# Attention batches 3 to 7: 32x32 block turns on VectorE in place of TensorE transposes, attention pieces behind the second product, and a later place for the pair splits

## The chip, the cores and the metric

The kernel runs on one core of one Trainium2 chip. The metric is device time in microseconds (us), of one launch. Engines are named as in the profile: PE is TensorE's matmul stream and PEld its weight loads, DVE is VectorE, ACT is ScalarE, POOL is GpSimd, SP is SyncE, which here issues every DMA.

## What is computed

Attention in both directions between 512 tokens and 32 states, in 8 batches of 8 heads, then two feed-forward blocks on the 8 x 544 = 4352 rows that result:

```python
scores = scale * x @ state.T          # (B,H,S,Ns) = (8,8,512,32), D = 64
a = softmax(scores, -1); xread = a @ state
a2 = softmax(scale * state @ x.T, -1); sread = a2 @ x
h0 = concat([xread, sread], axis=2)   # -> rows (4352, 512)
h1 = (relu(h0 @ w_in) ** 2) @ w_out   # w_in 512x2048, w_out 2048x512
out = (((h1 @ w1) * (h1 @ w2)) @ w3) @ w_out2
```

The weights arrive as 64-bit floats. Products run in the fp32r type, with each operand split into a high and a low part and three passes (HI,HI), (LO,HI), (HI,LO), so one product of a 128x128 weight tile takes three matmuls.

## The kernel before, in words

**First half: attention and the first block.** The work is cut into chunks c: chunks 0 to 7 are the 512 tokens of a batch, chunk 8 is the 256 state rows of all batches. For each of the 16 tiles f of 128 hidden columns, `h_tile(c, f)` (L375) makes the hidden tile with 6 matmuls of 512 columns (products of `SW`, which is state times w_in, with the turned attention weights `aT`), `act_h` (L367) does relu and square on ScalarE and the split into HI (ScalarE, L83) and LO (VectorE, L84), and `y_tile` (L410) adds the tile's part to the four output banks with 12 matmuls. `y_tile` runs two tiles behind `h_tile` (the list `pend`, L578). The main loop is at L558; its index i counts (c, f), and from i = 32 on i = 16 c + f.

Between `h_tile` and `y_tile` of iteration i the loop runs `side[i]` (L562), a table written by hand. For each batch b it holds, in the iterations of chunk b - 1: the attention pieces of batch b in the slots of `att_slots` (L336); `make_sw` (L349) in slots 1, 5, 9 and 13, 16 matmuls that fill the two banks of tag "m"; every second iteration one `conv`, which makes fp32 out of one 512 KB block of 64-bit weights with five VectorE instructions and one on ScalarE (`convert64`, L123), stores it, and loads a later block; and two x loads with their copies on GpSimd. The raw blocks and the raw x tiles share three buffers (tag "raw").

The attention pieces of one batch on TensorE are: `xpose` four times (four 128x128 transposes of x against the identity, L228), `scores` (16 matmuls into both "m" banks, L240), `soft1a` twice (four transposes of the scores S, so that the row softmax over the 32 states runs along a row, L268), `a_T` twice (four transposes back, L288), `a2_T` twice (L297), `sread` twice (16 small matmuls, L305) and `sread_T` twice (one transpose, L319). All use the two "m" banks. The slots are L340 to L345: xpose 0 to 3, scores 4, a2_T 6 and 10, soft1a 7 and 11, sread 8 and 11, sread_T 9 and 12, a_T 10 and 13.

`tc.issue_after(ins)` (L561) queues each instruction that the block traces on the engine of `ins` behind `ins`; here `done[i - 3]`, the VectorE half of a hidden tile's split. The rest of the order on each engine is made by the scheduler from the order of the program.

**Second half.** Eight token chunks go in four pairs, twice (s = 0 and 1, for the two halves of the 1024 columns; the second pass takes the pairs in reverse). For each pair `quad` (L714) runs four times, 42 matmuls each: seven products of sums and differences of the operands take the place of eight, and VectorE puts the results together. Then come eight output tiles `out_tile` (L793) of 12 matmuls. The operands Y of the next pair are loaded by `load_pair` (L667, two buffers of tag "wi1") and made by `make_pair` (L680): 14 splits, each one cast on ScalarE and one subtraction on VectorE (L84), and 8 differences on VectorE (L693). Chunks 0 and 1 were written in three parts, so for the pair (0, 1) `load_pair` also loads the other parts and adds them on GpSimd (L676). `load_pair` is called after quad m = 1 (L848), `make_pair` after the first output tile (L862). The scheduler may place the VectorE work of `make_pair` earlier than where it is called.

## Time and profile before

| | us |
|---|---|
| median of 3 runs (lowest, highest) | 1330.67 (1328.37, 1331.24) |
| the profiled execution, its own time | 1329.5 |
| its span, first to last instruction | 1327.7 |
| PE busy | 1284.6 (97%) |
| PEld busy | 1012.7 (76%) |
| DVE busy | 782.9 (59%) |
| ACT busy | 654.8 (49%) |
| POOL busy | 64.5 (5%) |
| DMA, share of the 16 engines' span | 30.5% |
| mean granted clock of TensorE | 0.985 |

The profiled execution is 1.2 us shorter than the median. Spans on TensorE are modelled and overlap, so the time of a piece is read here from the start of one instruction to the start of the next. The clock is a share of 2.4 GHz; 0.50 is 1.2 GHz.

### The profile page before, as it was taken

To read this page: it belongs to the slowest core of one execution; us is meant where nothing else is said; L and a number is where in the kernel's file an instruction comes from. 1 tells how busy PE (TensorE), PEld (TensorE's weight loads), DVE (VectorE), ACT (ScalarE), POOL (GpSimd) and SP (SyncE) were. 2 spreads that over 40 slices of the span, in tenths; PEclk is the share of its full clock that TensorE was granted. 3 is DMA by queue.
4 is the path that set the end of the run, shared out by engine and by line. 5 is a ranking of instruction groups with operands and counts; after the bars stand their busy time and mean duration, and the time that the engine had idled before them with its cause. 6 is when DMAs were issued, how large, how long until landed. Compare 5 with 4: busy or idle time off the path is not lost.

```text
span 1327.7 us, 17120 instructions
## 1 busy us (share of the span) xinstructions
PE 1284.6 (97%) x6552; PEld 1012.7 (76%) x6552; DVE 782.9 (59%) x1388; ACT 654.8 (49%) x1190; POOL 64.5 (5%) x52
## 2 busy tenths in 40 slices
PE   3998999999999999999999999999799999999998
PEld 2666677777777777777789988888688888888877
DVE  6899875565656656543244764736273747567552
ACT  3765765656556565554565633525153533425121
POOL 0112300000000000000000000000500000000000
PEclk8898999999999999999999999999899999999999
DMA  6246534233242332300031342031502235050322
GB/s 205 65 129 223 172 103 135 96 103 104 81 149 72 105 117 80 103 9 1 33 127 64 108 162 79 18 110 60 179 32 96 78 129 163 28 191 9 119 70 89
DMA packets 65361, 132.70 MB, mean 100 GB/s; under 512 B 8704, under 2 KB 17408, under 8 KB 64768
## 3 DMA queue, kind: packets, MB, share of 16 engines
q1 hardware_dynamic: 65280, 131.62, 30.5%
q8 instruction: 51, 0.84, 0.2%
q14 instruction: 30, 0.25, 0.1%
HBM read 88.08 MB, written 43.52 MB: 99 GB/s over the span
## 4 chain that ended last, share of the span: by engine, by line
PE 86%; DVE 7%; DMA 3%; ACT 2%; issue 1%; POOL 1%; SPq 0%; POOLq 0%; DVEq 0%
PE y L419 25%; PE po L799 12%; PE qa L718 9%; PE qd L718 6%; PE ps_sw L354 3%; PE ps_w L603 3%; PE qc L718 3%; PE qe L718 3%; PE ab L773 2%; DMA yp<-yscr 1%; PE ps_r L309 1%; PE ps_x L232 1%; DVE ce L143 1%; DVE cm L140 1%; DVE ghl L84 1%
## 5 line engine op out<-in xcount | busy, mean ns | idle before, releaser
L419 PE MATMUL y<-ghl,wo 128*128 128x512 f32 (+1 forms) x1728 | 414.6, 386 | 5.4 <-ACT yo L428 5.0
L419 PEld LDWEIGHTS y<-ghl,wo 128*128 128x128 f32 x1728 | 304.8, 189 | 103.2 <-issue 24.7
L84 DVE TENSOR_TENSOR ghl<-r,ghl 128x512 fp32r<-128x512 f32 (+1 forms) x144 | 96.8, 672 | 150.7 <-ACT ghl L83 129.9
L718 PE MATMUL qa<-yq,wq 128*128 128x512 f32 x576 | 144.9, 390 | 0.0
L726 ACT COPY s<-qa 128x512 f32<-128x512 f32 x96 | 56.4, 588 | 146.7 <-PE qa L718 141.0
L718 PEld LDWEIGHTS qa<-yq,wq 128*128 128x128 f32 x576 | 108.5, 188 | 22.7
L718 PE MATMUL qd<-yq,wq 128*128 128x512 f32 x384 | 99.5, 393 | 8.3 <-ACT s L726 8.3
L799 PE MATMUL po<-w34b,c 128*128 128x512 f32 x408 | 95.9, 390 | 0.3 <-DVE o L808 0.3
L799 PE MATMUL po<-w,c 128*128 128x512 f32 x408 | 95.6, 390 | 0.0
L718 PEld LDWEIGHTS qd<-yq,wq 128*128 128x128 f32 x384 | 72.8, 190 | 23.9 <-ACT s L726 8.7
L371 ACT ACTIVATE r<-r 128x512 f32<-128x512 f32 (+1 forms) x144 | 88.2, 612 | 2.3
L799 PEld LDWEIGHTS po<-w34b,c 128*128 128x128 f32 x408 | 76.3, 188 | 17.1 <-DVE o L808 0.8
L799 PEld LDWEIGHTS po<-w,c 128*128 128x128 f32 x408 | 76.2, 188 | 16.4 <-ACT o L805 0.8
L83 ACT CAST ghl<-r 128x512 fp32r<-128x512 f32 (+1 forms) x144 | 86.2, 599 | 3.3
L136 ACT ACTIVATE ce<-ce,ebias 128x512 int32<-128x512 int32 x72 | 51.9, 724 | 31.2 <-DVE ce L135 31.0
L354 PE MATMUL ps_sw<-win,stT 64*32 64x512 f32 (+1 forms) x528 | 55.9, 595 | 1.6 <-DVE aT L84 0.8
L730 DVE TENSOR_TENSOR s<-qa,s 128x512 f32<-128x512 f32 x32 | 22.1, 690 | 59.3 <-ACT s L726 59.3
L143 DVE SCALAR_TENSOR_TENSOR ce<-raw,ce 128x512 int32<-128x512 int32 x72 | 50.9, 708 | 4.1 <-ACT ce L136 4.0
L140 DVE SCALAR_TENSOR_TENSOR cm<-raw,cm 128x512 f32<-128x512 uint32 x72 | 52.9, 735 | 0.6
L83 ACT CAST c<-s 128x512 fp32r<-128x512 f32 x64 | 38.9, 621 | 28.8 <-DVE s L747 28.2
L83 ACT CAST yq<-yraw 128x512 fp32r<-128x512 f32 x70 | 42.1, 624 | 16.0 <-PE qa L718 7.5
L718 PE MATMUL qc<-yq,wq 128*128 128x512 f32 x192 | 50.0, 396 | 0.0
(542 smaller groups left out, 1851.0 us busy)
## 6 DMA issues: line engine op xcount, KB each, us to landing
raw<-in_moe_w_dram SPq DMA_DIRECT2D x32, 512.0 KB, 4.1
yraw<-yscr SPq DMA_DIRECT2D x56, 256.0 KB, 4.7
raw<-in_moe_w_out_dram SPq DMA_DIRECT2D x24, 512.0 KB, 3.7
yscr<-yo SPq DMA_DIRECT2D x48, 256.0 KB, 3.0
oscr<-o SPq DMA_DIRECT2D x34, 256.0 KB, 3.0
opart<-oscr SPq DMA_DIRECT2D x34, 256.0 KB, 3.5
x<-in_x_dram SPq DMA_DIRECT2D x16, 512.0 KB, 4.0
out_dram<-o SPq DMA_DIRECT2D x32, 256.0 KB, 2.8
```

Source lines behind the costliest of these rows:

```text
L83: nc.scalar.copy(hi, src)
L84: return nc.vector.tensor_tensor(out=lo, in0=src, in1=f32(hi), op=ALU.subtract)
L136: nc.scalar.activation(e, e, ACTF.Relu, bias=ebias, scale=8.0)
L140: nc.vector.scalar_tensor_tensor(out=f32(m), in0=lw, scalar=2.0**-32, in1=m, op0=ALU.mult, op1=ALU.add)
L143: nc.vector.scalar_tensor_tensor(out=e, in0=hw, scalar=-(2**31), in1=e, op0=ALU.bitwise_and, op1=ALU.bitwise_or)
L354: nc.tensor.matmul(pss[r][k * NS:(k + 1) * NS, cols], stT[rows, b, k, :], win_t[fg][rows, k, cols], start=True, stop=True, tile_position=( ...
L371: nc.scalar.activation(r[:, :n], r[:, :n], ACTF.Square)
L419: nc.tensor.matmul(y_ps[c, d][:, :n], wo_t[f][:, wi, d * P:(d + 1) * P], t[:, gi, :n], start=(f == f0 and k == 0), stop=(f == f1 - 1 and k ...
L603: nc.tensor.matmul(ps, t[:, wi, (j % 4) * P:(j % 4 + 1) * P], wo2_t[j][:, vi, :], start=(j == 0 and k == 0), stop=(j == N1 - 1 and k == 2),)
L718: nc.tensor.matmul(ps, W[w, kt][:, wi, m * P:(m + 1) * P], Y[v, kt][:, vi, :], start=(first and kt == 0 and k == 0), stop=(last and kt == ...
L726: nc.scalar.copy(t, ps)
L799: nc.tensor.matmul(ps, v[:, vi, t * P:(t + 1) * P], w[:, wi, :], start=(m == 0 and k == 0), stop=(m == QM - 1 and k == 2),)
```

## The change

For batches 3 to 7 (`b >= BLK`) x is loaded twice. `load_xb` loads it in pieces of 32 tokens by 32 columns, so that VectorE's 32x32 block transpose (`turn_x`) gives the turned x; `load_xn` loads it straight into the tile X that `sread` reads, with the tokens in natural order. `xpose`, its copies on ScalarE and GpSimd's copies of x go. `soft1a` turns S in 32x32 blocks on VectorE, which leaves the 32 states along the row, and `a_T` turns the weights back on VectorE, into the buffer of S. The slots are moved up, since no turn of x stands ahead of the scores. The output rows of chunks 3 to 7 are stored in natural order.

For batches 2 to 7 the attention pieces move from `side` to `late`: they are issued behind `y_tile` and not between `h_tile` and `y_tile`.

In the second half `load_pair` is called after quad m = 0, and what `make_pair` and `make_w` put on VectorE is queued behind the last VectorE instruction of the pair's quads.

```diff
@@ -54,6 +54,7 @@
     HI, LO = 0, 1
+    BLK = 3
@@ -217,6 +218,33 @@
+    xT = {}
+    def load_xb(b, g):
+        t = raw_tile(False, f"xb{b}_{g}").bitcast(F32).rearrange("p a b -> p (a b)")
+        for r in range(2):
+            for a in range(2):
+                p0 = (2 * r + a) * NS
+                for k in range(2):
+                    nc.sync.dma_start(
+                        t[p0:p0 + NS, k * 512:(k + 1) * 512].rearrange("p (c i) -> p c i", i=NS),
+                        x[b, g * HG + 2 * k + r, :, a * NS:(a + 1) * NS].rearrange("(c p) i -> p c i", p=NS),
+                    )
+        raws["xb", b, g] = t
+    def turn_x(b, g):
+        raw = raws.pop(("xb", b, g))
+        for k in range(2):
+            t = att.tile([P, 512], F32, tag="xT", bufs=4, name="xT")
+            nc.vector.transpose(out=t, in_=raw[:, k * 512:(k + 1) * 512])
+            xT[b, 2 * g + k] = t
+    def load_xn(b, g):
+        t = att.tile([P, HG, J, D], F32, tag="X", bufs=2, name=f"X{b}_{g}")
+        nc.sync.dma_start(t, x[b, g * HG:(g + 1) * HG].rearrange("h (j p) d -> p h j d", p=P))
+        X[b, g] = t.rearrange("p h j d -> p j h d")
@@ -235,7 +263,7 @@
             nc.scalar.copy(t, ps)
-            v["xT", k] = t
+            xT[b, k] = t
@@ -243,7 +271,7 @@
                     nc.tensor.matmul(
-                        pss[r][k * NS:(k + 1) * NS, :], stT[rows, b, k, :], v["xT", k][rows, :],
+                        pss[r][k * NS:(k + 1) * NS, :], stT[rows, b, k, :], xT[b, k][rows, :],
                         start=True, stop=True, tile_position=(r * D, k * NS),
@@ -266,13 +294,17 @@
         def soft1a(r):
-            ps = bank_m("ps_n")
-            for j in range(J):
-                nc.tensor.transpose(ps[:, j * P:(j + 1) * P], v["S", r][:, j * P:(j + 1) * P], ident)
-            pv = ps.rearrange("p (k n) -> p k n", n=NS)
+            e = att.tile([P, J * HG, NS], F32, tag="e1", bufs=1, name="e1")
+            if b >= BLK:
+                nc.vector.transpose(out=e.rearrange("p k n -> p (k n)"), in_=v["S", r])
+                pv = e
+            else:
+                ps = bank_m("ps_n")
+                for j in range(J):
+                    nc.tensor.transpose(ps[:, j * P:(j + 1) * P], v["S", r][:, j * P:(j + 1) * P], ident)
+                pv = ps.rearrange("p (k n) -> p k n", n=NS)
             mx = att.tile([P, J * HG, 1], F32, tag="mx", bufs=2, name="mx")
             nc.vector.tensor_reduce(out=mx, in_=pv, axis=AX.X, op=ALU.max)
-            e = att.tile([P, J * HG, NS], F32, tag="e1", bufs=1, name="e1")
             nc.vector.tensor_tensor(out=e, in0=pv, in1=mx.to_broadcast([P, J * HG, NS]), op=ALU.subtract)
@@ -286,10 +318,14 @@
         def a_T(r):
-            ps = bank_m("ps_a")
             e = v["e1", r].rearrange("p k n -> p (k n)")
-            for j in range(J):
-                nc.tensor.transpose(ps[:, j * P:(j + 1) * P], e[:, j * P:(j + 1) * P], ident)
+            if b >= BLK:
+                ps = v["S", r]
+                nc.vector.transpose(out=ps, in_=e)
+            else:
+                ps = bank_m("ps_a")
+                for j in range(J):
+                    nc.tensor.transpose(ps[:, j * P:(j + 1) * P], e[:, j * P:(j + 1) * P], ident)
             t = pa.tile([P, 2, 512], F32R, tag=f"aT{r}", bufs=2, name=f"aT{r}")
@@ -337,6 +373,12 @@
         xp, sc, s2, s1a, s1b, at, a2t, sr, srt = att_steps(b)
+        if b >= BLK:
+            return [
+                [sc], [], [s2[0], s1a[0]], [],
+                [s1b[0], s2[1]], [a2t[0]], [at[0], s1a[1]], [sr[0]],
+                [s1b[1], srt[0]], [a2t[1]], [at[1]], [sr[1]], [srt[1]], [], [], [],
+            ]
         return [
@@ -505,6 +547,7 @@
     side = {i: [] for i in range(NF * B)}
+    late = {}
     side[0] = [lambda: make_win0(1, 0), s2[0], lambda: make_win0(1, 1), xp1[0], xp1[1], a2t[0]]
@@ -521,13 +564,18 @@
         for i, steps in enumerate(att_slots(b)):
-            side[(b - 1) * NF + i] = steps + side[(b - 1) * NF + i]
+            late[(b - 1) * NF + i] = steps
         for fg in range(NFG):
...
             i = 9 + g if b == 2 else (b - 2) * NF + 12 + g
-            side[i].append(lambda b=b, g=g: (load_x(b, g), make_x(b, g)))
+            if b < BLK:
+                side[i].append(lambda b=b, g=g: (load_x(b, g), make_x(b, g)))
+            else:
+                side[i - 4].append(lambda b=b, g=g: load_xb(b, g))
+                side[i - 2].append(lambda b=b, g=g: turn_x(b, g))
+                side[i + 2].append(lambda b=b, g=g: load_xn(b, g))
     for _ in range(3):
@@ -578,6 +626,9 @@
             y_tile(*pend.pop(0))
+        with tc.issue_after(done[i - 3].ins) if i >= 8 else nullcontext():
+            for job in late.get(i, ()):
+                job()
@@ -708,8 +759,8 @@
         t = bp.tile([P, 2, 512], F32R, tag="c", bufs=2 * QM, name="c")
-        split(t[:, HI, :n], t[:, LO, :n], q)
         c_t[c, m] = t
+        return split(t[:, HI, :n], t[:, LO, :n], q)
@@ -748,7 +799,7 @@
         nc.vector.tensor_tensor(out=p1, in0=p1, in1=u3, op=ALU.mult)
-        to_c(c0, m, p1, 512)
+        return to_c(c0, m, p1, 512)
@@ -807,7 +858,8 @@
         if c < B:
-            dst = out[c * T:c * T + S, :].rearrange("(p j) e -> j p e", j=J)[t]
+            rows_t = "(p j) e -> j p e" if c < BLK else "(j p) e -> j p e"
+            dst = out[c * T:c * T + S, :].rearrange(rows_t, j=J)[t]
             nc.sync.dma_start(dst, o)
@@ -844,8 +896,8 @@
             for m in range(QM):
-                quad(c0, c1, m)
-                if m == 1 and i + 1 < len(todo):
+                last = quad(c0, c1, m)
+                if m == 0 and i + 1 < len(todo):
                     raw = load_pair(*todo[i + 1])
@@ -859,10 +911,11 @@
                 out_tile(c, t, s)
-                if n == 0 and i + 1 < len(todo):
-                    make_pair(raw)
-                if n == 0 and i + 1 == len(todo) and s == 0:
-                    make_w(raw)
+                with tc.issue_after(last.ins):
+                    if n == 0 and i + 1 < len(todo):
+                        make_pair(raw)
+                    if n == 0 and i + 1 == len(todo) and s == 0:
+                        make_w(raw)
                 if n == 3 and i + 1 == len(todo) and s == 1:
...
             if s == 0 and i + 1 == len(todo):
```

**How the order moves.** TensorE, tiles 0 to 2 of chunk 4, while batch 5's attention is worked on (ph is the hidden tile, y an output bank, ps_x the turned x, ps_s the scores, ps_sw the product of `make_sw`). Before:

```order
L383 MATMUL ph_0__3578<-aT_3340,sw_3494 128x512 x3
L383 MATMUL ph_0__3578<-aT_3481,sw_3497 128x512 x3
L232 MATMUL ps_x<-ident,X_0_3449 128x128 x4
L419 MATMUL y_2976<-ghl,wo_1648 128x512 x3
...
L383 MATMUL ph_1__3622<-aT_3340,sw_3494 128x512 x3
L383 MATMUL ph_1__3622<-aT_3481,sw_3497 128x512 x3
L232 MATMUL ps_x<-ident,X_0_3449 128x128 x4
L354 MATMUL ps_sw<-win_660,stT 32x512 x8
L419 MATMUL y_2976<-ghl,wo_1662 128x512 x3
```

Now:

```order
L425 MATMUL ph_0__3556<-aT_3166,sw_3472 128x512 x3
L425 MATMUL ph_0__3556<-aT_3365,sw_3475 128x512 x3
L461 MATMUL y_2969<-ghl,wo_1641 128x512 x3
...
L461 MATMUL y_2972<-ghl,wo_1641 128x512 x3
L273 MATMUL ps_s<-xT,stT 32x512 x8
L425 MATMUL ph_1__3607<-aT_3166,sw_3472 128x512 x3
L425 MATMUL ph_1__3607<-aT_3365,sw_3475 128x512 x3
L396 MATMUL ps_sw<-win_660,stT 32x512 x8
L461 MATMUL y_2969<-ghl,wo_1655 128x512 x3
```

The transposes are gone, the scores stand behind the output product, and a hidden tile stands between an attention piece and the next ps_sw.

VectorE in the second half, first pass, around the quads of the pair (6, 7), with what each row waits for (yraw, ytmp and yq belong to the splits of the next pair; s and c to the quads). Before:

```order
L84 TENSOR_TENSOR yq<-yraw,yq 128x512 [waits PE_49]
L693 TENSOR_TENSOR ytmp<-yraw 128x512 [waits Pool_49]
L693 TENSOR_TENSOR yraw<-yraw 128x512 [waits DVE_49,Pool_49]
L730 TENSOR_TENSOR s_8462<-qe,s_8462 128x512 [waits PE_49]
L730 TENSOR_TENSOR s_8485<-qd,s_8485 128x512 [waits PE_49,Activation_49]
L693 TENSOR_TENSOR ytmp<-yraw 128x512 [waits Pool_49]
L730 TENSOR_TENSOR s_8470<-qa,s_8470 128x512 [waits Activation_49]
```

Now:

```order
L801 TENSOR_TENSOR s_8608<-s_8608,s_8652 128x512 [waits DVE_49]
L85 TENSOR_TENSOR c<-s_8631,c 128x512 [waits Activation_49]
L85 TENSOR_TENSOR c<-s_8608,c 128x512 [waits Activation_49]
L85 TENSOR_TENSOR yq<-yraw,yq 128x512 [waits Pool_49] x2
L744 TENSOR_TENSOR ytmp<-yraw 128x512
L744 TENSOR_TENSOR ytmp<-yraw 128x512 [waits Pool_49]
```

The rows that wait for GpSimd stood among the first quad's rows; now they stand behind the last quad's two splits of c.

TensorE in the second pass, from a pair's first output tile to the next pair's quads (po is an output tile, qa, qd, qe and qc are the banks of a quad). Before:

```order
L799 MATMUL po<-w34b,c 128x512 x12
L718 MATMUL qd<-yq,wq 128x512 x3
L718 MATMUL qe<-yq,wq 128x512 x6
L799 MATMUL po<-w34b,c 128x512 x60
L718 MATMUL qa<-yq,wq 128x512 x6
```

Now:

```order
L850 MATMUL po<-w34b,c 128x512 x20
L769 MATMUL qa<-yq,wq 128x512
L850 MATMUL po<-w34b,c 128x512 x4
L769 MATMUL qa<-yq,wq 128x512 x4
L850 MATMUL po<-w34b,c 128x512 x12
L769 MATMUL qa<-yq,wq 128x512
L769 MATMUL qd<-yq,wq 128x512 x6
L769 MATMUL qe<-yq,wq 128x512 x6
L769 MATMUL qa<-yq,wq 128x512 x12
...
L850 MATMUL po<-w34b,c 128x512 x60
```

The whole first quad of the next pair now stands behind 36 matmuls of output tiles and ahead of the other 60; before, 9 matmuls of it stood there. In the first pass almost all of it stays behind all eight output tiles.

## Rows read from the trace of the kernel before

**Rows 1.** Profile page, part 1: busy us (share) x instructions, each engine.

```profile
PE 1284.6 (97%) x6552; PEld 1012.7 (76%) x6552; DVE 782.9 (59%) x1388; ACT 654.8 (49%) x1190; POOL 64.5 (5%) x52
```

**Rows 2.** Windows: stretch, us, busy PE PEld DVE ACT POOL (x), PEclk, DMA, GB/s.

```profile
131.50:216.20 84.70, 82.95 (x444) 60.77 (x444) 64.13 (x122) 53.72 (x97) 14.49 (x8) 1.00 0.43 141
216.20:624.60 408.40, 408.36 (x2212) 304.14 (x2211) 231.86 (x448) 237.23 (x417) 9.59 (x8) 1.00 0.28 88
624.60:694.30 69.70, 69.57 (x338) 54.22 (x337) 23.62 (x37) 39.37 (x68) 0.00 (x0) 1.00 0.21 76
```

**Rows 3.** Timeline of PE, chunk 4: start us, us; hidden tiles 1 to 14.

```profile
384.20 1.52 PE L383 MATMUL ph__3622<-aT,sw 128*128 128x512 f32 x6
...
390.76 1.52 PE L383 MATMUL ph__3682<-aT,sw 128*128 128x512 f32 x6
...
395.31 1.52 PE L383 MATMUL ph__3730<-aT,sw 128*128 128x512 f32 x6
...
399.87 1.52 PE L383 MATMUL ph__3762<-aT,sw 128*128 128x512 f32 x6
...
405.20 1.52 PE L383 MATMUL ph__3813<-aT,sw 128*128 128x512 f32 x6
...
410.55 1.53 PE L383 MATMUL ph__3865<-aT,sw 128*128 128x512 f32 x6
...
415.12 1.53 PE L383 MATMUL ph__3909<-aT,sw 128*128 128x512 f32 x6
...
419.69 1.52 PE L383 MATMUL ph__3954<-aT,sw 128*128 128x512 f32 x6
...
425.02 1.52 PE L383 MATMUL ph__4008<-aT,sw 128*128 128x512 f32 x6
...
431.15 1.53 PE L383 MATMUL ph__4053<-aT,sw 128*128 128x512 f32 x6
...
446.07 1.52 PE L383 MATMUL ph__4201<-aT,sw 128*128 128x512 f32 x6
...
453.01 1.52 PE L383 MATMUL ph__4254<-aT,sw 128*128 128x512 f32 x6
...
457.09 1.52 PE L383 MATMUL ph__4291<-aT,sw 128*128 128x512 f32 x6
```

**Rows 4.** Lines of DVE in chunk 4: count, busy us, mean ns, idle before.

```profile
L274 DVE TENSOR_REDUCE mx<-ps_n 128x16 f32<-128x512 f32 x2 | 1.4, 692 | 1.7 <-PE ps_n L271 1.7
```

**Rows 5.** Lines of POOL, whole span.

```profile
L176 POOL TENSOR_TENSOR wo<-cw,wo 128x512 fp32r<-128x512 f32 x16 | 25.9, 1618 | 99.3 <-ACT wo L175 89.5 <-DMA raw<-in_moe_w_in_dram 9.8
```

**Rows 6.** DMA queues, 1.5 to 4.0 us (only state loads): packets, MB, share.

```profile
q1 hardware_dynamic: 717, 0.16, 29.2%
```

**Rows 7.** Timeline of SP at the start: eight state loads.

```profile
0.74 3.69 SPq L440 DMA_DIRECT2D st<-in_state_dram  x8
```

**Rows 8.** Timeline of PE, chunk 1, with waits in brackets.

```profile
159.69 1.57 PE L354 MATMUL ps_sw<-win,stT 64*32 64x512 f32 x16 [0.71 <-ACT S L251]
...
166.57 0.66 PE L300 MATMUL ps_a<-ident,e 128*128 128x128 f32 x4 [0.98 <-DVE sw L84]
```

**Rows 9.** Windows of two pairs' periods in the second half, columns as in rows 2.

```profile
935.50:1006.70 71.20, 62.88 (x265) 51.34 (x264) 37.72 (x57) 26.72 (x48) 15.31 (x12) 0.93 0.37 118
1129.20:1189.10 59.90, 59.90 (x266) 49.56 (x264) 38.88 (x62) 20.83 (x38) 0.00 (x0) 1.00 0.33 106
```

**Rows 10.** Timeline of PE, first pass, quads of the pair (6, 7).

```profile
957.56 2.92 PE L718 MATMUL qd<-yq,wq 128*128 128x512 f32 x6 [8.32 <-ACT s L726]
```

**Rows 11.** Timeline of DVE in the same stretch.

```profile
953.67 0.69 DVE L693 TENSOR_TENSOR ytmp<-yraw 128x512 f32<-128x512 f32 x1 [8.83 <-POOL yraw L676]
```

**Rows 12.** Timeline of PE where the pair (4, 5) passes to output tiles.

```profile
912.26 4.24 PE L799 MATMUL po<-w,c 128*128 128x512 f32 x18
```

**Rows 13.** Timeline of DVE in the same stretch.

```profile
916.18 1.28 DVE L84 TENSOR_TENSOR c<-s,c 128x512 fp32r<-128x512 f32 x2
```

**Rows 14.** Windows: the end of the wait of rows 10 and what followed.

```profile
957.50:963.40 5.90, 5.84 (x14) 4.58 (x15) 3.44 (x4) 1.21 (x3) 2.42 (x3) 0.50 0.23 70
```

## The prediction

> **What bounds the kernel now.** I read the page's busy times first: TensorE is busy 97% of the span, the next engine 59% [rows 1]. What TensorE issues, and the few gaps in it, sets the time. Next the windows by stage: chunks 2 to 6, in which batches 3 to 7 get their attention, take 408.40 us, all of it TensorE busy, so 81.68 each; chunk 7, with no attention beside it, takes 69.70; chunk 1, with batch 2's attention, 84.70 [rows 2]. Attention therefore costs about 12 us a chunk on the engine that binds. Then TensorE's timeline of one chunk, read from one hidden tile's start to the next [rows 3]: the reader is to see that an iteration with nothing beside it lasts 4.08 us (453.01 to 457.09), and by how much each piece makes it longer. Last the second half: a pair's period is 59.90 us, one of them is 71.20 [rows 9].
>
> The sum below is made against the profiled execution's 1329.5 us. The median of the runs stands 1.2 higher, and I add that at the end. A measurement of this kernel can tell some 0.2% (2.7 us) from no change.
>
> **First half, batches 3 to 7.** Per batch 32 transposes leave TensorE: four groups of four for x, two for `soft1a`, two for `a_T`. One group costs 0.48 us (395.31 to 399.87 is 4.56, against 4.08) [rows 3]. Eight groups are 3.84 us.
>
> There is a second saving. A `make_sw` alone adds 1.27 us (405.20 to 410.55). Where it follows an attention piece directly, the two cost more than their sum, since both want the two "m" banks: with an x group 2.48 (384.20 to 390.76), 0.73 too much; with `sread_T`, taken as 0.12, a quarter of a group, 2.05 (425.02 to 431.15), 0.66 too much; with an `a_T` group 2.86 (446.07 to 453.01), 1.11 too much [rows 3]. That is 2.50 per batch. In the new order a hidden tile stands between an attention piece and each `make_sw`, and no piece follows another directly.
>
> What stays, built up from the plain chunk: 69.70 holds three `make_sw`; add a fourth (1.27), the scores (399.87 to 405.20, 1.25), two `a2_T` groups (410.55 to 415.12, 0.49 each), two `sread` (419.69 to 425.02, 1.25 each) and two `sread_T` (0.12 each): 75.94 us [rows 2, 3]. That is 5.74 less than 81.68, **28.7 us less in five chunks**. (The two savings add to 6.34; the plain chunk has 0.6 us of waits of its own, 69.70 less 16 x 4.08 and 3 x 1.27, which I leave in.)
>
> What could eat it:
> - *VectorE.* It gets eight block turns a batch. No row shows one. The ends are nothing and 1.62 us, the slowest 128x512 pass of any engine, GpSimd's subtraction [rows 5]. I take 0.69, VectorE's own row reduction, a pass of the same size with one source [rows 4]. VectorE is busy 231.86 / 5 = 46.4 us a chunk [rows 2]; with eight turns that is 51.9 of 75.9, with the upper end 59.3. It is covered; without cover it would cost its 5.5 us a batch. A turn would have to take 3.7 us before VectorE filled the chunk.
> - *The scores before a `make_sw`.* Both banks of the scores must be copied by ScalarE before the next `make_sw`, one hidden tile (1.36 of the 4.08) later. Between nothing and the 0.73 of the x group I take 0.3 a batch, **+1.5 us**.
> - *The x loads.* Each batch issues 16 block loads and two of X on SP in place of two. Eight small loads of the state hold SP 3.69 us [rows 7], so 16 hold it some 7.4, once a chunk, with weight loads and stores behind. The pieces are of 128 bytes, 4096 for each half of a batch. State pieces of 256 bytes take 29.2% of 16 engines over 2.5 us for 717, or 16.3 ns [rows 6]; 4096 of them are 4.2 us on 16 engines. The ends are half of that (half the bytes) and 20 us. I take 4.2 and cost it at nothing: the turn of the second half stands three hidden-tile splits later in VectorE's order than the conversion that frees its buffer, some 13 us.
> - *The Trainium skill, "DMA: Bandwidth & Descriptors", Specifications,* gives 512 bytes as the least size for full rate, below which the engine reads, modifies and writes. If that doubled a piece's time, a half would need 8.4 us, still inside the 13; the sum is the same by row and by rule, but this is why the last rival below gets 5% and not 2%.
> - ScalarE loses four copies a batch and GpSimd two; neither binds, so that gives nothing.
>
> **First half, batch 2.** It keeps its transposes, only behind the output product. Chunk 1 shows two plain waits, 0.71 and 0.98, of attention work for data that was not yet ready [rows 8], and has the same adjacent pieces as above, 2.50. At most 4.2 goes; the order is new, so nothing may go, or waits of the same 1.7 may appear. I take **-3.0 us**.
>
> **Second half.** The long period is that of the pair (6, 7): 71.20 against 59.90 [rows 9]. TensorE waits 8.32 us for ScalarE [rows 10], which waits for VectorE, which stands 8.83 us at a difference of the pair (0, 1) until GpSimd has added the parts [rows 11]. Afterwards the granted clock is 0.50, that is 1.2 GHz, for the rest of the first quad [rows 14]; six matmuls take 2.92 there. In the new order these differences stand behind the last quad's splits, so VectorE cannot be held inside the quads: **-11.3 us**. GpSimd's additions then have the whole 38 us of the quads; the load starts when `make_pair` of (6, 7) has freed its buffers.
>
> What is late next is `make_pair`. VectorE's last splits of c end at 917.46, 5.2 us after the quads [rows 12, 13]. Behind them come 22 instructions, at 0.64 each (1.28 for two) [rows 13] 14.1 us, so the last operand is ready 19 us after the quads. In the first pass eight output tiles, 96 matmuls at 0.227 (18 in a plain iteration of 4.08) [rows 3], cover 21.8 us, which is enough. In the second pass the next quad starts after only 42 matmuls, 9.5 us. It asks for its operands in the order in which they are made and needs the last kind some 8 us in, at 17.7 us. So up to 1.5 us is late, perhaps nothing, perhaps 2.5 with the output additions in between. I take 0.6 for each of three such passages: **+1.8 us**.
>
> **Sum.** 1329.5 - 28.7 + 1.5 - 3.0 - 11.3 + 1.8 = 1289.8; with the 1.2 to the median, **1291.0 us**.
>
> **The rivals.**
> 1. *Collisions move and do not go.* The pieces behind the output product hold the "m" banks just as long; the scores come closer to a `make_sw`, and VectorE empties other banks later in a fuller queue. Then the 2.50 a batch stays, and batch 2 gains nothing: 1291.0 + 12.5 + 3.0 - 1.5 = **1305**. For it: the waits of rows 8 are of this kind. Against it: a whole hidden tile now stands in between.
> 2. *The passages in the second pass bind.* If each makes TensorE wait 4 us, at the ratio of the known wait (11.3 lost for 8.32) that is 16.3 in place of 1.8: **1305.5**. For it: the order puts a whole quad early. Against: operands come in the order of use.
> 3. *Slower.* The block loads land so late that VectorE stands at a turn, with the hidden tiles' splits behind it. TensorE has two tiles in hand, 8 us, on top of the 13. With a wait like the known one in each of five batches the cost is 56.5: **1347.5**. To lose all of the 39.7 gained, a batch must lose 7.9, a wait of 5.8 at that ratio, so a half must land over 27 us after its issue, more than six times the 4.2.
>
> That the change does not do what it says can be left out: the rows of the new order show the transposes gone and the pieces moved.
>
> **How the numbers follow.** My forecast 0.69 (1283 to 1299), rival 1 0.15, rival 2 0.09, rival 3 0.05, something that cancels the gain almost exactly 0.02. The lower end, 1283, is the sum without the two allowances (3.3), with batch 2's full 4.2 and the plain chunk's own waits gone (3.0). The upper end takes in rivals 1 and 2 and half of their overlap: 1309. Faster by over 0.2%: 0.93; within: 0.02; slower: 0.05.
>
> **What would show it.** Right: no TensorE rows of x turns in chunks 2 to 6, each of these chunks near 76 us, block turns near 0.7, `make_sw` iterations near 5.35 everywhere, no pair's period above 61 us, clock 1.00 through the second half. Wrong: chunks of 78 or more with all transposes gone (rival 1), 62 to 66 us periods in the second pass (rival 2), or VectorE waiting for x loads in the list of waits (rival 3).

## The result and the profile after

The changed kernel takes **1299.22 us** (median of 4 runs, 1298.32 to 1300.17), the kernel before 1330.49 in the runs beside it: ratio 0.9768, 95% interval 0.9751 to 0.9785. That is 31.3 us less. The forecast was 39.7 less and 1291.0; the time lies 8 us above it, inside the range of 1283 to 1309.

The profiled execution took 1299.79 us, its span 1298.0. Page, part 1, and the windows of the stretches that [rows 2] show of before (chunk 1, chunks 2 to 6, chunk 7):

```profile
PE 1255.5 (97%) x6392; PEld 988.4 (76%) x6392; DVE 801.2 (62%) x1428; ACT 651.6 (50%) x1170; POOL 57.4 (4%) x42
```
```profile
132.70:222.80 90.10, 85.22 (x459) 61.09 (x458) 67.35 (x125) 55.71 (x99) 12.04 (x6) 0.98 0.51 139
222.80:602.10 379.30, 377.60 (x2035) 284.23 (x2034) 247.04 (x484) 228.28 (x395) 0.00 (x0) 1.00 0.40 106
602.10:671.80 69.70, 69.60 (x337) 54.21 (x337) 23.62 (x37) 39.20 (x68) 0.00 (x0) 1.00 0.23 76
```

Chunks 2 to 6 went from 408.40 to 379.30, chunk 7 did not move, and **chunk 1 grew**, from 84.70 to 90.10. Chunks 3 to 6 are 76.06 each; chunk 2 is 75.09, because the scores of batch 3 (1.0) have moved ahead of its first hidden tile. Like for like, chunk 1 is 4.4 longer and five chunks 28.1 shorter. Chunk 1 differs between executions: in three others with this first half (experiments 8 to 10) it is 90.3, 91.0 and 92.3.

TensorE's timeline of chunk 4, the starts of hidden tiles as in [rows 3]:

```profile
373.96 1.52 PE L425 MATMUL ph__3556<-aT,sw 128*128 128x512 f32 x6
...
379.15 1.65 PE L425 MATMUL ph__3607<-aT,sw 128*128 128x512 f32 x6
...
384.61 1.52 PE L425 MATMUL ph__3660<-aT,sw 128*128 128x512 f32 x6
...
393.39 1.52 PE L425 MATMUL ph__3742<-aT,sw 128*128 128x512 f32 x6
397.47 1.52 PE L425 MATMUL ph__3796<-aT,sw 128*128 128x512 f32 x6
...
403.33 1.64 PE L425 MATMUL ph__3844<-aT,sw 128*128 128x512 f32 x6
```

An empty iteration is 4.08 still (393.39 to 397.47). Scores and the `make_sw` after them take 5.19 and 5.46, together 2.49 more than two empty ones, no more than their own 1.25 and 1.27. A `make_sw` with an `a2_T` behind the output product adds 1.78 (397.47 to 403.33), their sum of 1.76 again. No piece pays for its neighbour any more. The turns, in VectorE's lines of chunks 2 to 6:

```profile
L240 DVE STREAM_TRANSPOSE xT<-xb 128x512 f32<-128x512 f32 x16 | 10.8, 697 | 0.1
L324 DVE STREAM_TRANSPOSE S<-e 128x512 f32<-128x512 f32 x10 | 7.1, 705 | 0.0
L299 DVE STREAM_TRANSPOSE e<-S 128x512 f32<-128x512 f32 x10 | 7.0, 703 | 0.0
```

Now chunk 1. One wait of TensorE stands out; its timeline, then those of ScalarE and VectorE, and the window behind it:

```profile
158.18 1.09 PE L273 MATMUL ps_s<-xT,stT 64*32 64x512 f32 x16
159.20 1.65 PE L425 MATMUL ph__1553<-aT,sw 128*128 128x512 f32 x6
164.31 2.44 PE L396 MATMUL ps_sw<-win,stT 64*32 64x512 f32 x16 [3.46 <-ACT S L279]
```
```profile
159.97 0.61 ACT L176 CAST wo<-cw 128x512 fp32r<-128x512 f32 x1
163.15 0.62 ACT L176 CAST wo<-cw 128x512 fp32r<-128x512 f32 x1 [2.57 <-DVE cw L147]
163.67 1.06 ACT L279 COPY S<-ps_s 128x512 f32<-128x512 f32 x2
```
```profile
161.56 1.56 DVE L147 SCALAR_TENSOR_TENSOR cw<-cm,ce 128x512 f32<-128x512 f32 x1
```
```profile
164.40:167.80 3.40, 3.40 (x19) 1.21 (x20) 2.33 (x8) 3.37 (x8) 0.72 (x1) 0.50 0.03 11
```

The scores of batch 2 begin at 158.18, and the hidden tile behind them at 159.20. The two copies of S that free the "m" banks stand on ScalarE behind two casts of converted weights; the second waits 2.57 us for VectorE's conversion. `make_sw`, the next to want the banks, starts 3.46 us late, and for 3.4 us after it the granted clock is 0.50. In the order before, the copies stood ahead of those casts. The Trainium skill, "PSUM — Partial Sum Buffer", Engine vs sequencer instructions, says that ScalarE's queue is strictly first in, first out; the copies' start at 163.67, behind a cast that had nothing to do with them, agrees.

The second half, against 59.90 and 71.20 in [rows 9]. Each window goes from one pair's first output tile to the next pair's. The second one holds the quads of the pair (6, 7), where the long wait was, the third those of the pair (0, 1); the last three are the second pass:

```profile
829.90:889.90 60.00, 60.00 (x265) 49.33 (x264) 34.00 (x54) 26.42 (x46) 0.00 (x0) 1.00 0.21 70
889.90:949.90 60.00, 60.00 (x265) 49.34 (x264) 36.32 (x54) 26.43 (x46) 21.79 (x16) 1.00 0.42 132
949.90:1010.20 60.30, 60.30 (x265) 49.23 (x265) 34.00 (x54) 24.03 (x42) 0.00 (x0) 1.00 0.20 70
1070.20:1132.10 61.90, 60.58 (x265) 48.97 (x265) 38.80 (x62) 21.78 (x38) 0.00 (x0) 1.00 0.31 102
1132.10:1193.20 61.10, 60.64 (x266) 48.97 (x265) 38.80 (x62) 21.77 (x38) 0.00 (x0) 1.00 0.31 104
1193.20:1253.60 60.40, 60.40 (x266) 48.92 (x265) 38.80 (x62) 18.34 (x32) 0.00 (x0) 1.00 0.23 74
```

The long period is gone and the clock is 1.00 in all of them; the one behind it is 60.3, and the three periods of the second pass have grown by 2.0, 1.2 and 0.5.

### The profile page after: what moved, and what is told of

It reads as the page before. It is cut to its first block, busy times and chain, and to the rows that moved or that the text cites. A ratio compares the mean times of both kernels' runs of the same rounds, so it can differ in the third digit from the quotient of the medians.

```text
span 1298.0 us, 16933 instructions
## 1 busy us (share of the span) xinstructions
PE 1255.5 (97%) x6392; PEld 988.4 (76%) x6392; DVE 801.2 (62%) x1428; ACT 651.6 (50%) x1170; POOL 57.4 (4%) x42
## 4 chain that ended last, share of the span: by engine, by line
PE 83%; DVE 8%; DMA 4%; ACT 3%; issue 1%; SPq 0%; POOL 0%; DVEq 0%; ACTq 0%; POOLq 0%
PE y L461 24%; PE po L850 12%; PE qa L769 10%; PE qd L769 6%; PE ps_w L654 3%; PE qc L769 3%; PE qe L769 3%; PE ps_sw L396 2%; PE ab L824 2%; PE ps_r L345 1%; DMA out_dram<-o 1%; DMA x<-in_x_dram 1%; DVE ghl L85 1%; DVE sw L85 1%; DMA yscr<-yo 1%
## 5 line engine op out<-in xcount | busy, mean ns | idle before, releaser
L461 PE MATMUL y<-ghl,wo 128*128 128x512 f32 (+1 forms) x1728 | 408.5, 383 | 8.9 <-ACT yo L470 7.7
L461 PEld LDWEIGHTS y<-ghl,wo 128*128 128x128 f32 x1728 | 309.6, 189 | 101.1 <-ACT r L411 17.6
L727 POOL TENSOR_TENSOR yraw<-yraw,yp 128x512 f32<-128x512 f32 x16 | 21.8, 1362 | 760.5 <-DMA oscr<-o 745.6
L859 DVE TENSOR_TENSOR o<-po,opart 128x512 f32<-128x512 f32 x34 | 23.4, 690 | 46.4 <-PE po L850 35.9
L141 DVE SCALAR_TENSOR_TENSOR cm<-raw,cm 128x512 f32<-128x512 uint32 x72 | 49.9, 693 | 0.8
```

The source lines that it names most:

```text
L141: nc.vector.scalar_tensor_tensor(out=f32(m), in0=lw, scalar=2.0**-32, in1=m, op0=ALU.mult, op1=ALU.add)
L461: nc.tensor.matmul(y_ps[c, d][:, :n], wo_t[f][:, wi, d * P:(d + 1) * P], t[:, gi, :n], start=(f == f0 and k == 0), stop=(f == f1 - 1 and k ...
```

## The experiments

Times are medians; each run had the kernel before beside it (1329.7 to 1330.6). "Chunk" lengths are those from one chunk's first hidden tile to the next one's, read from the trace.

**1 and 2. The wait in chunk 1.** First, the order of the casts alone:

```diff
+    s_copy = {}
...
-                nc.scalar.copy(s, pss[r])
+                s_copy[b] = nc.scalar.copy(s, pss[r])
...
-            for job in side.get(i, ()):
-                job()
+            with tc.issue_after(s_copy[2].ins) if i == 22 else nullcontext():
+                for job in side.get(i, ()):
+                    job()
```

> The changed kernel with one order added: the two weight conversions of iteration 22 are queued on ScalarE behind batch 2's two copies of S. Theory A (chunk 1 grew because those copies stood behind two casts of weights that wait for VectorE, so that make_sw found its banks full for 3.5 us and the clock then fell): TensorE's wait of 3.46 us at 161 us goes, no clock of 0.50 follows, chunk 1 goes from 90.1 to about 84.6, the kernel from 1299.2 to about 1293.7. Rival (the late place of batch 2's pieces costs by itself, or the block loads and turns of batch 3 that begin in chunk 1 do): another wait takes its place, chunk 1 stays within 1.5 of 90, the kernel at 1298 to 1299.

Second, batch 2's pieces back in their old place:

```diff
-            late[(b - 1) * NF + i] = steps
+            if b < BLK:
+                side[(b - 1) * NF + i] = steps + side[(b - 1) * NF + i]
+            else:
+                late[(b - 1) * NF + i] = steps
```

> The changed kernel with batch 2's pieces back between hidden tile and output product; batches 3 to 7 as changed. Theory A: the scheduler's old order comes back with the old place, the copies of S ahead of the casts, chunk 1 about 85 to 86 (84.7 as before, and 1.0 for batch 3's scores if they stay there), the kernel 1294 to 1295. Rival (block loads and turns of batch 3 in chunk 1): they are still there, chunk 1 stays at 89 to 90, the kernel at 1299.

Windows of chunk 1, of the first and then of the second:

```profile
132.40:217.60 85.20, 83.20 (x460) 60.59 (x459) 67.14 (x126) 55.21 (x99) 12.02 (x6) 1.00 0.52 148
```
```profile
132.60:220.80 88.20, 85.80 (x459) 61.28 (x458) 66.29 (x125) 54.72 (x99) 11.81 (x6) 1.00 0.51 144
```

The first gives 1292.80 us (ratio 0.9717, 0.9702 to 0.9731): chunk 1 goes from 90.1 to 85.2, the wait and the clock of 0.50 are gone. Theory A holds: about 5 us of the miss is the place of two casts. The second gives 1294.49, but its chunk 1 is 88.2, not the 85 to 86 expected: the old waits of [rows 8] are back (0.8 and 1.0), and something new remains near its end. So the late place itself is good for batch 2, and there is a second loss.

**3. The second loss: scores drawn forward.** In chunk 1 of experiment 1 the scores of batch 3 take 3.65 us in place of 1.02, behind an `a_T` of batch 2, and 42 matmuls of the output product follow in a row. The edit queues these scores behind the output product:

```diff
...
-            y_tile(*pend.pop(0))
+            y_last = y_tile(*pend.pop(0))
...
-            for job in late.get(i, ()):
-                job()
+            with tc.issue_after(y_last.ins) if i == 32 else nullcontext():
+                for job in late.get(i, ()):
+                    job()
```

> The first experiment's kernel (conversions of iteration 22 behind the copies of S) with a second order: on TensorE the scores of batch 3 stand behind the output product that is written ahead of them. Theory A2 (what is left of the miss in chunk 1 is that these scores were drawn forward by more than one hidden tile, directly behind an a_T of batch 2 that holds the same banks: 3.65 us for what takes 1.02): the collision of 2.6 goes, 1.0 moves from chunk 1 to chunk 2, chunk 1 goes from 85.15 to about 81.5 and chunk 2 from 75.1 to 76.1, the kernel from 1292.8 to about 1290.2. Rival (the scores are late there because their operands are, and would wait as long in any place): 85.15 + 75.08 = 160.2 stays within 0.7, the kernel at 1292.8.

1292.74 us, no change; chunks 1 and 2 are 159.6 in place of 160.2. The rival was right: the time is waited for elsewhere, now in the output product. TensorE's timeline:

```profile
200.59 0.96 PE L462 MATMUL y<-ghl,wo 128*128 128x512 f32 x3 [1.16 <-ACT yo L471]
202.61 9.14 PE L462 MATMUL y<-ghl,wo 128*128 128x512 f32 x39 [1.06 <-DVE yo L469]
```

Two output banks had not been copied out (`yo`, two buffers). Why is on SyncE, whose timeline in the changed kernel reads (there all of this stands some 6 us later than in the run above):

```profile
182.35 14.56 SPq L230 DMA_DIRECT2D xb<-in_x_dram  x16
197.01 0.91 SPq L471 DMA_DIRECT2D yscr<-yo  x2
```

The first two copies are done at 190.5 (ScalarE 188.83, VectorE 189.82), and their stores wait behind sixteen block loads until 197.0. The other two copies need the same buffers; in the order that was made around this they stand on ScalarE and VectorE behind the splits of aT and two block turns, at 206.0 and 208.0. Before the change these stores were issued from 184.73 on, as soon as the first copy (184.10, 0.60 long) had ended.

**4. The loads off SyncE.** On top of experiment 1:

```diff
-                    nc.sync.dma_start(
+                    (nc.gpsimd if b == 3 else nc.sync).dma_start(
```

> The first experiment's kernel (conversions of iteration 22 behind the copies of S) with the sixteen block loads of batch 3 issued by GpSimd in place of SyncE. Theory A3 (they hold SyncE for 14.2 us, the stores of the output copies yo behind them go 7 us late, the two copies that need the same buffers stand 14 us late behind the splits of aT and the block turns, and their output banks hold TensorE up, first in the scores of batch 3 and, when these were moved, in the output product itself): the stores go within 2 us of their copies, the output products no longer bunch (42 in a row), no wait of the scores or of the output product above 0.8 from 195 us on; chunks 1 and 2 together go from 160.2 to about 157.6, the kernel from 1292.8 to about 1290.2. Rival (a_T of batch 2 and the scores of batch 3 collide in the m banks whatever SyncE does): chunks 1 and 2 stay at 160, the kernel at 1292.8. Other rival (loads issued by GpSimd land late and the turns hold VectorE): a wait of VectorE for xb, 1294 or more.

SyncE, and the window of chunk 1:

```profile
183.16 3.16 SPq L472 DMA_DIRECT2D yscr<-yo  x3
...
189.09 0.32 SPq L472 DMA_DIRECT2D yscr<-yo  x1
```
```profile
132.20:214.50 82.30, 79.79 (x443) 59.93 (x442) 67.20 (x125) 54.63 (x97) 22.45 (x22) 1.00 0.52 157
```

The stores follow their copies, the output products no longer bunch, and the scores are back in chunk 2 (76.05). Chunks 1 and 2 are 158.4, 1.8 less than in experiment 1 and not the 2.6 expected: one output product still waits 1.6 us at 187 us for a `yo` copy, which waits for the buffer of the store before. And only half of the 1.8 belongs to the loads. TensorE, in experiment 1 and then here, at an earlier wait for a `yo` copy, at batch 2's scores, and at the second hidden tile of chunk 2, which in both stands behind batch 3's scores:

```profile
147.24 1.79 PE L462 MATMUL y<-ghl,wo 128*128 128x512 f32 x6 [1.59 <-ACT yo L471]
158.31 1.09 PE L274 MATMUL ps_s<-xT,stT 64*32 64x512 f32 x16
221.64 1.52 PE L426 MATMUL ph__2175<-aT,sw 128*128 128x512 f32 x6
```
```profile
146.27 1.70 PE L462 MATMUL y<-ghl,wo 128*128 128x512 f32 x6 [0.87 <-ACT yo L471]
157.25 1.09 PE L274 MATMUL ps_s<-xT,stT 64*32 64x512 f32 x16
219.70 1.65 PE L426 MATMUL ph__2175<-aT,sw 128*128 128x512 f32 x6
```

The first wait is over before any block load is issued (from 177 us on), and it differs from execution to execution whatever the order (1.42 in experiment 12, which has both repairs). From the scores to the hidden tile it is 63.33 in experiment 1 and 63.36 in experiment 3, against 62.45 here and 62.5 in experiments 11 and 12. So **the loads on SyncE cost 0.9**. The run does not separate their hold on the queue from the order that the scheduler made around it. In time it is 1291.69 against 1292.80, which the intervals (0.9690 to 0.9723, 0.9702 to 0.9731) do not separate; the traces do.

**5 and 6. The two savings apart.** All pieces back in `side` (block turns alone); and `BLK = B` (late pieces alone):

> The changed kernel with all attention pieces back between hidden tile and output product: block turns alone. Theory C (two savings, transposes 3.84 a batch and collisions 2.5 a batch): the transposes stay gone, and of the collisions come back those of pieces that now stand directly ahead of a make_sw, the two a2_T at some 0.7 each: chunks 3 to 6 about 77.5 each in place of 76.06, the kernel 7 us above what chunk 1 leaves. Rival (block turns give nearly all): chunks stay within 0.5 of 76.06. Other rival (the late place gives most): chunks above 79.

> The changed kernel with no block turns (BLK = B): all batches transpose on TensorE, all from batch 2 on with their pieces behind the output product. Theory C: chunks 3 to 6 are 75.94 + 3.84 = 79.8, and up to 0.7 more where two pieces share a slot. Rival (no collision goes by the late place, only the transposes did it): 81.7 as before. Other rival (a wait of make_sw for the copies of S as in chunk 1, in each batch): 84 or more.

Windows of chunks 2 to 6, of the first and then of the second:

```profile
220.10:611.20 391.10, 387.65 (x2035) 286.31 (x2034) 246.97 (x484) 228.34 (x395) 0.00 (x0) 1.00 0.37 103
```
```profile
222.10:618.40 396.30, 396.28 (x2211) 300.86 (x2210) 235.25 (x448) 240.70 (x417) 8.81 (x8) 1.00 0.28 90
```

Late pieces alone bring chunks 3 to 6 from 81.7 to 79.3 (-2.4 each), block turns alone to 78.66 (-3.0), both to 76.06 (-5.6). The two add up. Neither rival holds. Late alone came out 0.5 below the 79.8 expected, with no loss in shared slots. With the turns alone chunks are 1.2 longer than the 77.5 expected: TensorE's window there shows 387.65 busy of 391.10, 3.45 of waiting in five chunks against 1.70 in the changed kernel, so a third of it is waiting; the rest stays open. The kernels take 1307.11 (1306.70 and 1307.52) and 1316.72 (1315.68 and 1317.77).

**7. VectorE's cover.** Each block turn done twice:

> The changed kernel with each block turn done twice in a row into the same tile: eight more passes of 0.70 us a batch on VectorE. Theory D (VectorE's time is covered in chunks 2 to 6): VectorE's busy time rises by 5.6 to about 58 of 76 us a chunk, the chunks stay at 76.06 within 0.3, the kernel at 1299 to 1300. Rival (turns stand on the path where the scores or the splits of aT wait for them): 0.7 or more for each turn on the path, chunks at 77 to 81, the kernel 5 to 25 us slower.

1299.72 us. Windows of chunk 3, first of the changed kernel, then of this one:

```profile
298.00:374.00 76.00, 75.70 (x412) 56.83 (x411) 52.26 (x104) 46.26 (x80) 0.00 (x0) 1.00 0.48 125
```
```profile
298.70:374.70 76.00, 75.70 (x411) 56.88 (x410) 57.09 (x111) 46.21 (x80) 0.00 (x0) 1.00 0.46 125
```

VectorE is 4.8 us busier, TensorE's stretch is the same. Theory D holds: VectorE's part costs nothing here, and twice of it would not.

**8 to 10. The second half taken apart.** The changed kernel with one thing altered: the first pass alone as changed (8); `load_pair` after quad 1 again, `make_pair` still queued (9); `load_pair` early, `make_pair` not queued (10).

```diff
-                if m == 0 and i + 1 < len(todo):
+                if m == s and i + 1 < len(todo):
...
-                with tc.issue_after(last.ins):
+                with tc.issue_after(last.ins) if s == 0 else nullcontext():
```
```diff
-                if m == 0 and i + 1 < len(todo):
+                if m == 1 and i + 1 < len(todo):
```
```diff
-                with tc.issue_after(last.ins):
+                with nullcontext():
```

> The changed kernel with the old place of load_pair and make_pair in the second pass; the first pass as changed. Theory B (the splits of the next pair, queued behind the quads, stand ahead of the output additions on VectorE): the second pass returns to periods of 59.9 from 61.9, 61.0 and 60.4, 3.7 us in all, the first pass stays at 60.0, the kernel goes to about 1295.5. Rival (SyncE's queue, where load_pair now waits with stores behind it): the same here; the next run tells them apart.

> The changed kernel with load_pair called after quad 1 again in both passes; the splits still queued behind the last quad. Theory B: the periods of the second pass stay at 61.9, 61.0 and 60.4, within 0.5 each, the kernel at 1299. Rival (SyncE's queue): the second pass returns to about 59.9 a period, the kernel to 1295.5. In the first pass both expect the pair (6, 7) within 1 us of 60.3.

> The changed kernel with load_pair early (after quad 0) but make_pair not queued behind the quads, so that the scheduler may draw its VectorE work into the quads as before. Theory E (the wait of 8.8 us came from where VectorE's differences stand; the early load alone does not move them off the quads): the period of the pair (6, 7) stays above 64, up to 71, the second pass returns to 59.9, the kernel at 1299 to 1308. Rival (the parts came late, and one quad earlier, 9.4 us, is enough): that period is 60 to 61, the kernel at 1295 to 1297 with the second pass at 59.9.

Run 10, the period of the pair (6, 7), and VectorE inside it:

```profile
890.50:962.00 71.50, 62.27 (x266) 50.62 (x265) 36.14 (x55) 25.54 (x47) 20.88 (x16) 0.93 0.36 111
```
```profile
932.29 0.69 DVE L744 TENSOR_TENSOR ytmp<-yraw 128x512 f32<-128x512 f32 x1 [8.05 <-POOL yraw L727]
```

Run 10 (1307.61) has the old wait in full: the load one quad earlier does nothing by itself. Run 9 (1298.70) has 60.0 in this stretch, as the changed kernel has. So **the place of the 22 VectorE instructions gives the 11 us**, without the early load.

What the early load gives is not shown. Behind that stretch, in the quads of the pair (0, 1), run 9 has 61.3 and the changed kernel 60.3, but eight executions with the changed second half spread from 60.0 to 61.1 there. The wait, in TensorE's and ScalarE's lines of run 9, is not for a pair's parts:

```profile
980.35 1.66 PE L769 MATMUL qd<-yq,wq 128*128 128x512 f32 x6 [1.05 <-ACT s L777]
```
```profile
979.20 0.62 ACT L84 CAST wq<-wraw 128x512 fp32r<-128x512 f32 x1 [3.35 <-DMA wraw<-w12s]
979.72 0.58 ACT L777 COPY s<-qd 128x512 f32<-128x512 f32 x1
```

A copy that empties a bank stands on ScalarE behind a cast of the second pass's weights, which waits for its load: the pattern of chunk 1 once more. In the changed kernel the same cast waits 2.29.

For the second pass, run 8 returns to 60.21, 59.86 and 59.87 (1297.02, ratio 0.9739 to 0.9772, where 1295.5 was expected; its runs spread from 1295.23 to 1299.44). Run 9 came out at 60.4, 60.4 and 60.4, which neither theory had. So did the kernel of experiment 2, whose second half is the changed one's: a queued `make_pair` costs 0.5 a passage, and the further 1.5 and 0.6 of the profiled execution are not in every execution. There VectorE's output additions waited for a store of `o` to leave its buffer:

```profile
1092.30 0.69 DVE L859 TENSOR_TENSOR o<-po,opart 128x512 f32<-128x512 f32 x1 [1.71 <-DMA out_dram<-o]
1095.52 0.69 DVE L859 TENSOR_TENSOR o<-po,opart 128x512 f32<-128x512 f32 x1 [2.54 <-DMA out_dram<-o]
...
1104.38 0.69 DVE L859 TENSOR_TENSOR o<-po,opart 128x512 f32<-128x512 f32 x1 [3.54 <-DMA out_dram<-o]
```

They come bunched, since nearly all of `make_pair` (1074.86 to 1089) stands ahead of all but one. The same order stands in experiments 2 and 9, which have one such wait there, of 1.72 and 1.75, and periods of 60.4, so the order alone does not make the others. Why the stores leave late in some executions, and whether `load_pair`'s place has a part in it, stays open.

**11 and 12. The repairs together.** Experiments 1, 4 and 8:

> The changed kernel with three repairs: conversions of iteration 22 behind the copies of S, block loads of batch 3 on GpSimd, and the old place of load_pair and make_pair in the second pass. Theories A, A3 and B add: the previous kernel's 1290.2, less 0.5 for each of the three passages of the second pass (60.4 against 59.9), and less the waits for stores of o that single executions show there: 1287 to 1289. Rival (the parts share a limit, or the second pass was as fast in the mean): 1290 to 1291.

1291.01 us, the rival's time. The second pass has 59.9 three times, but the passage into it 62.08: VectorE stands in a quad at a difference whose part was loaded late, behind the loads of w34b on SyncE:

```profile
1038.46 0.69 DVE L746 TENSOR_TENSOR yraw<-yraw 128x512 f32<-128x512 f32 x1 [5.45 <-DMA yraw<-yscr]
```

The last run has the early load in both passes and queues `make_pair` in the first alone:

> The previous repairs of the first half (conversions of iteration 22 behind the copies of S, block loads of batch 3 on GpSimd), and in the second half make_pair queued behind the quads in the first pass alone, with load_pair after quad 0 in both passes. Theory F (in the earlier joint run the period of 62.08 came from the late load: VectorE stood 5.45 us at a difference whose part was still behind the loads of w34b on SyncE): with the load one quad earlier no period of the second pass is above 60.1, the first pass is as in the changed kernel (60.0, 60.0, 60.6, 60.0), the kernel goes to about 1289.5, 1.5 below the joint run. Rival (the wait is that of the unqueued differences, whenever the load is issued): one period of the second pass or the passage into it stays at 61 to 62, the kernel at 1291.

1289.65 us (5 runs, 1289.37 to 1292.15; ratio 0.9703, 0.9690 to 0.9717). The periods of the second pass are 59.95, 59.87 and 59.87; the passage into it is 60.71, with 0.4 of waiting, more than the 60.1 said and far less than 62.08. It is 0.7% faster than the changed kernel, and the fastest here; that it is faster than the joint run before is within the spread of the runs.

## Why the prediction was right, and where it was 8 us short

By the profiled executions (span 1327.7 to 1298.0, 29.7 less where 39.7 was forecast), chunk 1 fell short by 7.4, the second half by 2.2, and the five chunks gave 0.9 more than the two terms together. The last 1.2 or so stands ahead of chunk 1, which begins at 132.7 instead of 131.5; in the other runs it begins between 130.8 and 133.2, so that is spread. Term by term:

- **Batches 3 to 7: -28.7, and +1.5 allowed.** Measured -28.1 like for like. The chunk came out at 76.06 where 75.94 was built up, so the allowance for scores ahead of a `make_sw` was needed for 0.12 of its 0.3 at most. The split holds too: collisions 2.50 forecast, 2.4 alone and 2.6 on top of the turns measured (experiments 5 and 6); transposes 3.84, less the 0.6 of waits that were left in (put on this side here), 3.24 forecast, 3.0 alone and 3.2 on top of the late pieces measured.
- **VectorE covers the turns.** Right, and shown by doubling them. A turn takes 0.70 where 0.69 was taken.
- **Batch 2: -3.0.** This step failed: +4.4. Its upper end, "waits of the same 1.7 may appear", looked at TensorE's order alone. The pieces that free TensorE's banks stand in ScalarE's, VectorE's and SyncE's queues, and there chunk 1 differs from the later chunks: it converts two blocks of weights in some iterations. The copies of S behind two casts cost 4.9 of the chunk's length (experiment 1; 5.4 from batch 2's scores on, 68.71 against 63.33), the block loads ahead of the `yo` stores 0.9 (experiment 4). With both put right, chunk 1 is 82.3 to 83.1 in three executions, 1.6 to 2.4 less than before; most of the gain that the step forecast was there, and two queues ate it.
- **The x loads, costed at nothing.** The landing was right: sixteen loads in a batch land 2.3 us after issue each, and VectorE does not wait for them. The hold on SyncE was estimated at 7.4 us from the state loads; it is 14.2. In chunks 2 to 6 nothing that TensorE waits for stands behind it; in chunk 1 the `yo` stores do. The prediction named the stores and did not ask which of them would be late.
- **Second half: -11.3 and +1.8.** Measured -7.3 (first output tile of the first pair to the end: 475.4 before, 468.1 now). The long period went as forecast, by the step named (experiment 10). The passages were sized well, 0.5 for the 0.6 taken; the 2.1 beyond that, and some 0.4 in the period behind that of (6, 7), were missed. This execution is the slowest here: in seven others with the same second half the same stretch takes 466.0 to 467.3, so that there the forecast of -9.5 is missed by 0.1 to 1.4 only.

Of the rivals, none came as told: the chunks of 78 or more that rival 1 asked for are not there, though its condition, banks emptied later in a fuller queue, is what struck in chunk 1, on ScalarE where the rival named VectorE. Rival 2's periods of 62 to 66 were nearly reached once, at 61.9; no period above 61 had been expected, and there were two. The order rows of one plain chunk told the truth for five chunks; the chunk that was left out of them held most of the miss.

That the time lies inside the range is in part luck. The forecast's own part of it ended at 1299, where the time fell; what lies above, up to 1309, was put there for rivals 1 and 2, and neither is what happened. (How 1309 follows is not shown; both rivals in full would give 1319.5.)

## What to carry to other kernels

When pieces move on the engine that binds, look up in the other engines' rows where the instructions stand that free its buffers, in every stage and above all in the one that is not like the rest: an in-order queue with something slow ahead of a freeing copy costs as much as a missing operand (5 us in chunk 1, and 1 us in the quads of experiment 9). Count a transfer's issue time on its queue as an instruction's, and name the stores behind it. And queue work that waits for others behind the last instruction of the critical product: that alone took 11 us out of a pair's period.

## What the runs showed of the hardware

- A load of 512 pieces of 128 bytes (64 KB) holds SyncE 0.89 us (sixteen: 14.23), one of the 512 KB loads of weights mostly 0.33 to 0.43. Issued by GpSimd in experiment 4, eight of the small-piece loads take 5.29 us, 0.66 each. The Trainium skill, "DMA: Bandwidth & Descriptors", Anatomy of one DMA, calls the generation of descriptors small, with many of them free, in the path that GpSimd issues; here it was not, on SyncE or on GpSimd.
- The pieces themselves are cheap. While only block loads moved (262.5 to 276.4 us, DMA queues):

```profile
q1 hardware_dynamic: 7062, 0.88, 39.4%
```

  39.4% of 16 engines over 13.9 us for 7062 pieces is 12.4 ns each, less than the 16.3 of the 256-byte state pieces [rows 6]. The doubling that the prediction weighed from the Trainium skill, "DMA: Bandwidth & Descriptors", Specifications, is not seen.
- A wait of 3.5 us was followed by 3.4 us at a granted clock of 0.50, which is 1.2 GHz: `make_sw` and the output product behind it, 2.37 and 3.35 us from start to start, take 1.02 and 2.86 in the first experiment, where nothing waits.
